# Converting three pairs of first-layer weights at double width, earlier, with the attention's slots moved around it

## The chip, the core and the metric

One core of a Trainium2 chip runs the whole program. The metric is the device time of one execution in microseconds. Three runs of the kernel before are known, and one more execution was profiled.

## What is computed

A chunked attention, then two gated layers one after the other:

```python
# attention: 4 batches x 8 heads x 768 positions, head width 64,
# chunks of 32 queries see 8 memory keys and up to 56 neighbouring keys
out = softmax(q @ k.T / 8) @ v
x = out as 3072 tokens x 512
# first layer (d_ff 1024)
h = (x @ w1) * (x @ w2)
y = (h @ w3) @ w_out
# second layer (d_ff 1536)
return ((y @ w_a) * (y @ w_b)) @ w_out2
```

The weights arrive as 64-bit floats, each as two 32-bit words.

## The kernel before

The program has three stages on one core, and five engines share it: TensorE (PE) multiplies, VectorE (DVE), ScalarE (ACT) and GpSimd (POOL) do the rest, SyncE (SP) starts most transfers. Each engine works off its instructions strictly in the order in which the program issued them, and that order is written out by hand.

**The weights' phase** multiplies w3 by w_out once, so that the first layer needs only one matrix after the gate. It has two halves of four accumulator banks. Each half loops over `k` from 0 to 5 and inside over `m` from 0 to 3, then over `m` with `k` 6 and 7 together. When a bank is complete, `w_evict` (line 568) splits it into a high part (ACT) and a low part (DVE) in `wsm`. All four banks of a half must be evicted before the next half reuses them.

**The first layer** runs in six tiles of 512 tokens. `ab_step` forms eight gated blocks per tile (matmuls into `psA` and `psB`, a product `gv`, a high part on ACT, a low part on POOL), then four outputs `psY`. After each group of twelve matmuls `between` (line 643) is called: 24 steps per tile (`NB`).

**The second layer** follows in tiles, with weights that the earlier steps converted and stored.

Into the first two stages two other streams are woven.

The *conversion*: `w_tick` (line 409) advances a pipe of weight blocks by one stage. An item is loaded by SP (`w_load`), scaled by two ACT instructions (`w_scale`), assembled by three DVE instructions (`w_bits`, lines 383 to 385), and, for the first layer's weights, split into a high part (ACT, line 419) and a low part (DVE, line 413). One tick does the low part of one item, the high part of the next, the assembly of the one behind it and the scaling of the fourth. The plan holds 12 items of w3 and w_out, each 1024 wide, and then 16 items of w1 and w2, each 512 wide; a pair `m` is two of these. There are three ticks ahead of the weights' phase, eight in each half, and the rest happen one per step in the first tile.

The *attention*: 64 units `u` of 96 queries and four heads. `attn_slot` works off numbered slots. Unit u has its scores (`sc`, PE) in slot 3u, the maximum (`mx`, DVE) in 3u+1, the exponentials (`t`, ACT, line 209) in 3u+2, the sum's reciprocal (`sm`, DVE) and the normalisation (`t`, POOL, line 222) in 3u+3. Its transposition (`pt`, PE) lies in `trans_slot(u)`, the copy to `p` (ACT, line 234) one slot later; for odd units the product with v (`xp`, PE) and the split into the layer's input `xt` (ACT and DVE) follow one and two slots after that, or with `e` = 1 one later still. `NEED[i]` is the slot number by which tile i's input is complete: 42, 72, 102, 138, 168, 198. Within a tile the slots are spread over the 24 steps between `NEED[i]` and `NEED[i+1]`.

Slots in the second half, by (k, m), before: k 0: 19, 20 | 21, 22; k 1: 23 | 24, 25; k 2: 26, 27 | 28, 29; k 3: 30 | 31, 32; k 4: 33, 34 | 35, 36; k 5: 37 | 38, 39; then 40 and 41. Left of the bar stands what is issued after `m` = 1, right of it what is issued after `m` = 3, behind that step's tick. Counted from the first, tick 12 is the one at k 0 and tick 17 the one at k 5; ticks 18 and 19 stand with k 7.

Loads of units up to 13 are started by POOL (`queue_of`), later ones by SP, where they stand in line with the weight loads.

Of the kernel before, what the change touches and what calls it, by code (L numbers as in the profile page):

```python
# [7 lines left out]
F32 = mybir.dt.float32  # L8
F32R = mybir.dt.float32r
U32 = mybir.dt.uint32  # L10
# [3 lines left out]
P = 128  # L14
# [10 lines left out]
NPLAIN = 22  # L25
NEARLY = 14
# [3 lines left out]
KD = DM // P  # L30
M1 = DF1 // P
M2 = DF2 // P
NEG = -1.0e30
CH = 512
BUFS = {"raw64": (3, 0), "raw2": (0, 3), "dec": (2, 4)}
A0 = (1, 2)
TB = 2

# [5 lines left out]
def tile_attention_moe(  # L44
# [21 lines left out]
    wpool = ctx.enter_context(tc.tile_pool(name="wpool", bufs=8))  # L66
    xpool = ctx.enter_context(tc.tile_pool(name="xpool", bufs=2))
    stagestack = ExitStack()
    stage = stagestack.enter_context(tc.tile_pool(name="stage", bufs=2))
    p0stack = ExitStack()  # L70
    p0 = p0stack.enter_context(tc.tile_pool(name="p0", bufs=3))
# [203 lines left out]
    def trans_slot(u):  # L275
        return 3 * u + 5 + max(0, (NEARLY - 2 - u) // 2)

    def slots_of(u):
        t, e = trans_slot(u), int(u < NEARLY - 4)
        return (  # L280
            (t + 3 + e, a_x),
            (t + 2 + e, a_pv),
            (t + 1, a_pt),
            (t, a_trans),
            (3 * u + 3, a_norm),
            (3 * u + 2, a_exp),
            (3 * u + 1, a_max),
            (3 * u, a_scores),
        )
# [7 lines left out]
    acount = [-3]  # L297
    NSLOT = 3 * (NU - 1) + 9

    NEED = [3 * (2 * -(-TT * (i + 1) // GQ) - 1) + 9 for i in range(NT1)]  # L300

    def attn_slot(n=1):
        for _ in range(n):
            s = acount[0]
            if s >= NSLOT:
                return
            acount[0] += 1
            for _, u, stage_of in sorted(todo.get(s, []), key=lambda x: x[:2]):
                stage_of(u)

            if s % 3 == 1 and s // 3 + 1 > NPLAIN + 1:
                a_prep_lo(s // 3 + 1)
            if s % 3 == 2 and s // 3 + 2 > NPLAIN + 1:
                a_prep_hi(s // 3 + 2)
            if s % 3 == 0 and NPLAIN <= s // 3 + 1 <= NPLAIN + 1:
                a_prep_hi(s // 3 + 1)
            if s % 3 == 1 and NPLAIN <= s // 3 + 1 <= NPLAIN + 1:
                a_prep_lo(s // 3 + 1)
            if s % 3 == 0 and s // 3 + 2 >= NPLAIN + 2:
                a_load(s // 3 + 2)  # L320
            if s % 3 == 2:
                if s // 3 + 2 <= NPLAIN + 1:
                    a_load(s // 3 + 2)

    plan = []
    for k in range(8):
        plan += [("w3a", k, 0, w3a[k].rearrange("p a c -> p (a c)"))]
    c12 = [("w12", m, c, w12[m, :, c]) for m in range(M1) for c in range(2)]  # L330
    for k in range(4):
        plan += [("w3b", k, 0, w3b[k].rearrange("p a c -> p (a c)"))]
    plan += c12
    wsrc = [x[3] for x in plan]
    size = [1 if x[0] == "w12" else 2 for x in plan]
    NW0 = max(i for i, x in enumerate(plan) if x[0] == "w3b") + 1
    wraw = []
    nload = [0]

    turn = {tag: [0, 0] for tag in BUFS}  # L340
    live = {tag: [0, 0] for tag in BUFS}

    def w_tile(i, tag, shape):
        x = int(tag == "raw2")
        if i < NW0 and tag == "dec":

            x = int(turn[tag][1] * BUFS[tag][0] < turn[tag][0] * BUFS[tag][1])
        n = BUFS[tag][x]
        if live[tag][x] == n:
            return None, x  # L350
        turn[tag][x] += 1
        live[tag][x] += 1
        return (stage, p0)[x].tile(shape, U32, tag=tag, bufs=n, name=tag), x

    def w_load():
        i = nload[0]
        if i < len(wsrc):
            tag = "raw64" if size[i] == 1 else "raw2"
            r, x = w_tile(i, tag, [P, size[i] * CH, 2])
            if r is not None:  # L360
                for c in range(2 if i == 0 else 1):
                    n = size[i] * CH // (2 if i == 0 else 1)
                    nc.sync.dma_start(
                        out=r[:, n * c : n * c + n, :].rearrange("p c w -> p (c w)"),
                        in_=wsrc[i][:, 2 * n * c : 2 * n * c + 2 * n],
                    )
                nload[0] += 1
                wraw.append((i, r, tag))
                return True
        return False  # L370
# [20 lines left out]

    def w_sum(i, r):
        kind, f = plan[i][:2]
        if kind == "w12":
            a, ax = w_tile(i, "dec", [P, CH])
            w_bits(a, r)
            return a.bitcast(F32), ax
        if f % 2 == 0:
            pairs["f"] = wpool.tile([P, 2, 2 * CH], U32, tag="w12", name="w3_f")
        a = pairs["f"][:, f % 2, :]  # L400
        for a1, r1 in halves_of(i, a, r):
            w_bits(a1, r1)
        if kind == "w3a":
            w3k[f], wo_f[f] = a[:, :CH], a[:, CH:]
        else:
            w3k[8 + 2 * f], w3k[9 + 2 * f] = a[:, :CH], a[:, CH:]
        return None, None

    def w_tick():

        if len(pipe[2]):
            i, a, ax, (d, f, w, hi, lo) = pipe[2].pop(0)
            nc.vector.tensor_tensor(lo, a, hi.bitcast(F32), ALU.subtract)
            live["dec"][ax] -= 1
            d[f] = w
        if pipe[1]:
            i, a, ax = pipe[1].pop(0)
            t = w_place(*plan[i][:3])
            nc.scalar.activation(t[3], a, AF.Copy)
            pipe[2].append((i, a, ax, t))  # L420
        if len(pipe[0]):
            i, r, tag = pipe[0].pop(0)
            a, ax = w_sum(i, r)
            live[tag][int(tag == "raw2")] -= 1
            if ax is not None:
                pipe[1].append((i, a, ax))
        if wraw:
            i, r, tag = wraw.pop(0)
            for (r1,) in halves_of(i, r):
                w_scale(r1)  # L430
            pipe[0].append((i, r, tag))
        while w_load():
            pass
# [8 lines left out]

    def w_place(kind, m, c):

        if c == 0:
            pairs[kind] = wpool.tile([P, 2, 2 * CH], F32R, tag="w12", name="w12")
        w = pairs[kind][:, :, CH * c : CH * (c + 1)]
        v = pairs[kind].rearrange("p l (k j f) -> p l k j f", k=KD, j=2)
        return (w12s if c else {}), m, v, w[:, 0, :], w[:, 1, :]
# [118 lines left out]
    def w_evict(half, m):  # L568
        w = wsm[4 * half + m] = w_new(wpool, "wo")
        nc.scalar.activation(w[:, 0, :], banks[m], AF.Copy)  # L570
        nc.vector.tensor_tensor(w[:, 1, :], banks[m], w[:, 0, :].bitcast(F32), ALU.subtract)
# [3 lines left out]
    for half in range(2):  # L575
        banks = [psd.tile([P, 512], F32, tag="d", name="wps") for _ in range(4)]
        for k, m in order:
            mm(
                banks[m],
                w3k[8 * half + k].bitcast(F32)[:, P * m : P * m + P],  # L580
                wo_f[k].bitcast(F32),
                k == 0,
                k == 7,
            )
            if k < 6 and m % 2 == 0 or k == 6:
                continue

            if half == 0:
                if m == 1 or k == 7 and m == 3:
                    w_tick()  # L590
                attn_slot(A0[m // 2] * (k > 0) if k < 6 else 1)
            else:
                if k < 6:
                    if m == 3:
                        w_tick()
                    attn_slot(1 + (m == 3 or k % 2 == 0))
                else:
                    if m % 2 == 1:
                        w_tick()
                    if m < 2:  # L600
                        attn_slot()
            if k == 7 and m > 0:
                w_evict(half, m - 1)
        w_evict(half, 3)
    nc.sync.dma_start(out=mask_sb, in_=mask)
    del pairs["f"]
    wo_f.clear()
# [16 lines left out]
    def ab_step(w, rhs, g2, between):  # L624
# [11 lines left out]
        nc.scalar.activation(g2[:, 0, :], gv, AF.Copy)  # L636
        nc.gpsimd.tensor_tensor(g2[:, 1, :], gv, g2[:, 0, :].bitcast(F32), ALU.subtract)  # L637

    nstep = [0]

    NB = 2 * M1 + 2 * KD

    def between():
        nstep[0] += 1
        if any(pipe) or wraw:
            w_tick()
        else:
            n = 1
            if ti == NT1 - 1:
                b = nstep[0] - NB * ti  # L650
                n = 2 if b <= 2 * M1 - 1 else 3 * (2 * M1 < b <= 2 * M1 + 5)
            for _ in range(n):
                next(cw, None)
        if ti < NT1 - 1:
            b = nstep[0] - NB * ti
            attn_slot(NEED[ti] + (NEED[ti + 1] - NEED[ti]) * b // NB - acount[0])


    def tmp():
# [357 lines left out]
```

## Time and profile before

| what | value |
|---|---|
| runs | 1124.27, 1123.73, 1122.76 us; median 1123.73 |
| profiled execution | 1123.1 us, span 1121.3 us |
| PE busy | 1100.3 us, 98% of the span |
| DVE, ACT, POOL busy | 624.8, 515.7, 296.0 us |
| granted TensorE clock, mean | 0.995 |

The span is what the trace covers; the profiled execution's time is 1.8 us longer. Busy shares are averages over all stages. A granted clock of 1.00 is 2.4 GHz, 0.50 is 1.2 GHz.

### The profile page before, as it was taken

What the parts mean: (1) busy time and instruction counts of PE and PEld (TensorE: products, weight loads), DVE (VectorE), ACT (ScalarE), POOL (GpSimd) and SP (SyncE); (2) the same over time, 40 slices, a digit from 0 to 9 for tenths busy, and PEclk for the clock granted to TensorE, in tenths of its full rate; (3) what the DMA queues carried; (4) which work ended last, traced back from release to release, by engine and by line L of the source; (5) the groups of instructions that cost most, each with busy time, mean ns of one, the idle gap of its engine ahead of it and who ended that gap; (6) DMA issues with size and microseconds to landing.
All of it is one profiled execution on the core that took longest, in us unless ns stands there. A gap on an engine that the chain in (4) does not pass through costs nothing.

```text
span 1121.3 us, 15493 instructions
## 1 busy us (share of the span) xinstructions
PE 1100.3 (98%) x5354; PEld 876.6 (78%) x5354; DVE 624.8 (56%) x1342; ACT 515.7 (46%) x1299; POOL 296.0 (26%) x308
## 2 busy tenths in 40 slices
PE   8899999999999999999999999999999999999998
PEld 3456877877887878877877878888888888888887
DVE  7879955876986876855865564252232243222220
ACT  6777756666775756644543334232222223222210
POOL 3452232331331322311212233202233211232210
PEclk9999999999999999999999999999999999999999
DMA  8845445345345444436546455434334352344311
GB/s 304 282 126 175 123 150 181 122 141 184 115 146 191 134 142 150 148 113 198 176 163 234 169 188 192 170 99 169 132 137 180 143 178 91 145 143 186 132 38 37
DMA packets 61671, 174.55 MB, mean 156 GB/s; under 512 B 8022, under 2 KB 18080, under 8 KB 55577
## 3 DMA queue, kind: packets, MB, share of 16 engines
q1 hardware_dynamic: 48762, 102.38, 27.4%
q0 software_dynamic: 12544, 70.91, 17.6%
q8 instruction: 42, 0.69, 0.3%
q14 instruction: 36, 0.29, 0.1%
q10 hardware_dynamic: 287, 0.27, 0.1%
HBM read 139.97 MB, written 33.55 MB: 155 GB/s over the span
## 4 chain that ended last, share of the span: by engine, by line
PE 77%; DVE 3%; issue 3%; ACT 3%; DMA 1%; POOL 1%; DVEq 0%; ACTq 0%; POOLq 0%; SPq 0%
PE ps L803 29%; PE ops L92 17%; PE psA L92 10%; PE psB L92 9%; PE psY L92 9%; PE sc L92 2%; PE xp L92 1%; PE pt L230 1%; DMA wc<-co 1%; ACT t L209 1%; DVE dec L384 1%; POOL g L637 0%; POOL t L222 0%; ACT xt L143 0%; ACT q L143 0%
## 5 line engine op out<-in xcount | busy, mean ns | idle before, releaser
L803 PE MATMUL ps<-x,w 128*128 128x512 f32 x1512 | 349.5, 390 | 3.8 <-ACT tmp L815 3.8
L803 PEld LDWEIGHTS ps<-x,w 128*128 128x128 f32 x1512 | 283.4, 188 | 64.6 <-ACT tmp L815 5.9
L820 DVE TENSOR_TENSOR tmp<-ps,tmp 128x512 f32<-128x512 f32 x108 | 74.6, 690 | 245.3 <-PE ps L803 241.3
L92 PE MATMUL psA<-xt,w 128*128 128x512 f32 x576 | 146.6, 402 | 1.9 <-ACT xt L143 1.2
L92 PE MATMUL psY<-g,wo 128*128 128x512 f32 x576 | 139.8, 394 | 1.5 <-POOL g L637 1.5
L92 PE MATMUL psB<-xt,w 128*128 128x512 f32 x576 | 141.0, 393 | 0.0
L702 POOL DMA_DIRECT2D w<-wc x72 | 40.0, 557 | 369.3 <-PE ps L803 369.2
L815 ACT ACTIVATE tmp<-ps 128x512 f32<-128x512 f32 x108 | 64.4, 596 | 147.4 <-PE ps L803 145.2
L92 PEld LDWEIGHTS psA<-xt,w 128*128 128x128 f32 x576 | 107.1, 191 | 26.9 <-ACT xt L143 2.3
L92 PEld LDWEIGHTS psY<-g,wo 128*128 128x128 f32 x576 | 105.4, 188 | 23.6 <-POOL g L637 2.9
L92 PEld LDWEIGHTS psB<-xt,w 128*128 128x128 f32 x576 | 105.5, 188 | 21.0
L92 PE MATMUL ops<-wo,g 128*128 128x512 f32 x504 | 118.6, 389 | 0.0
L637 POOL TENSOR_TENSOR g<-gv,g 128x512 fp32r<-128x512 f32 x48 | 65.8, 1371 | 199.5 <-ACT g L636 199.4
L222 POOL TENSOR_TENSOR t<-t,sm 96x512 f32<-96x512 f32 x64 | 69.0, 1078 | 176.7 <-ACT k L143 81.2
L92 PEld LDWEIGHTS ops<-wo,g 128*128 128x128 f32 x504 | 94.6, 188 | 19.6
L826 ACT ACTIVATE g<-tmp 128x512 fp32r<-128x512 f32 x66 | 40.7, 633 | 130.1 <-DVE tmp L825 130.1
L827 POOL TENSOR_TENSOR g<-tmp,g 128x512 fp32r<-128x512 f32 x66 | 87.0, 1340 | 26.3 <-ACT g L826 25.6
L92 PE MATMUL ops<-fo,g 128*128 128x512 f32 x288 | 68.2, 389 | 0.0
L209 ACT ACTIVATE t<-t,mx 96x128 f32<-96x128 f32 x168 | 65.1, 390 | 5.6 <-DVE mx L194 5.6
L92 PE MATMUL wps<-w_f 128*128 128x512 f32 x128 | 60.9, 608 | 3.7 <-DVE w_f L385 1.9
L92 PEld LDWEIGHTS ops<-fo,g 128*128 128x128 f32 x288 | 54.1, 188 | 11.2
L636 ACT ACTIVATE g<-gv 128x512 fp32r<-128x512 f32 x48 | 30.2, 629 | 70.3 <-DVE gv L635 69.9
(83 smaller groups left out, 1303.9 us busy)
## 6 DMA issues: line engine op xcount, KB each, us to landing
w<-wc POOLq DMA_DIRECT2D x36, 1024.0 KB, 6.8
w<-wc POOLq DMA_DIRECT2D x36, 768.0 KB, 4.9
wc<-co SPq DMA_DIRECT2D x84, 256.0 KB, 2.5
raw<-in_wab SPq DMA_DIRECT2D x24, 512.0 KB, 4.3
kraw<-in_kt SPq DMA_DIRECT2D x42, 256.0 KB, 3.0
raw<-in_w SPq DMA_DIRECT2D x16, 512.0 KB, 4.1
raw<-in_w3a SPq DMA_DIRECT2D x7, 1024.0 KB, 8.8
vraw<-in_vw SPq DMA_DIRECT2D x50, 128.0 KB, 2.9
```

Source lines behind the costliest of these rows:

```text
L92: nc.tensor.matmul(o, lhsT=l, rhs=r, start=first, stop=last)
L209: nc.scalar.activation(t[:, h, :], src[:, h, :], AF.Exp, bias=mx[:, h : h + 1], scale=scale, accum_out=sm[:, h : h + 1],)
L222: nc.gpsimd.tensor_tensor(t, t, sm[:, :, None].to_broadcast([GQ, HH, KW]), ALU.mult)
L230: nc.tensor.transpose(pt[:, h, :], t[:, h, :], id_sb)
L636: nc.scalar.activation(g2[:, 0, :], gv, AF.Copy)
L637: nc.gpsimd.tensor_tensor(g2[:, 1, :], gv, g2[:, 0, :].bitcast(F32), ALU.subtract)
L702: nc.gpsimd.dma_start(out=t[:, c0:c1].bitcast(F32), in_=src[:, c0:c1])
L803: nc.tensor.matmul(ps, lhsT=w[:, i, a, k, :], rhs=xs[i][:, b, k, :], start=first and n == 0, stop=n == 5, skip_group_check=not first,)
L815: nc.scalar.activation(z, ps, AF.Copy)
L820: nc.vector.tensor_tensor(z, ps, y, ALU.add)
L826: nc.scalar.activation(g2[:, 0, :], z, AF.Copy)
L827: nc.gpsimd.tensor_tensor(g2[:, 1, :], z, g2[:, 0, :].bitcast(F32), ALU.subtract)
```

## The change

Three pairs of the first layer (`EARLY`, kind `w12p`) become three items 1024 wide, which use the wide raw buffers and two wide `dec2` buffers. The plan has 25 items in place of 28. The ticks keep their number up to the first tile; there, every third step has none. `w_evict` moves ahead of the tick and the slots of its step, and the last tick of the first half moves behind the last eviction. In the second half the slots become k 1: 23, 24 | 25, 26; k 2: 27 | 28, 29; k 4: 33 | 34, 35; k 5: 36, 37 | 38, 39. Units 12 to 19 get `e` = 1. The spread over the tiles goes by `AIM`: 42, 74, 106, 138. In the diff a line of dots marks what is left out (the bookkeeping of buffers).

```diff
-BUFS = {"raw64": (3, 0), "raw2": (0, 3), "dec": (2, 4)}
+BUFS = {"raw64": 3, "raw2": 3, "dec": 2, "dec2": 2}
+EARLY = 3
...
-        t, e = trans_slot(u), int(u < NEARLY - 4)
+        t, e = trans_slot(u), int(u < NPLAIN - 2 and u // 2 != NEARLY // 2 - 2)
...
-    for k in range(4):
-        plan += [("w3b", k, 0, w3b[k].rearrange("p a c -> p (a c)"))]
-    plan += c12
+    plan += [("w3b", k, 0, w3b[k].rearrange("p a c -> p (a c)")) for k in range(4)]
+    plan += [("w12p", m, 0, w12[m].rearrange("p a c -> p (a c)")) for m in range(EARLY)]
+    plan += [("w12", m, c, w12[m, :, c]) for m in range(EARLY, M1) for c in range(2)]
...
-            a, ax = w_tile(i, "dec", [P, CH])
+            tag = "dec" if size[i] == 1 else "dec2"
+            a = w_tile(tag, [P, size[i] * CH])
...
+        if kind == "w12p":
+            t = wpool.tile([P, 2, 2 * CH], F32R, tag="w12", name="w12")
+            v = t.rearrange("p l (k j f) -> p l k j f", k=KD, j=2)
+            return w12s, m, v, t[:, 0, :], t[:, 1, :]
...
+            if k == 7 and m > 0:
+                w_evict(half, m - 1)
             if half == 0:
-                if m == 1 or k == 7 and m == 3:
+                if m == 1:
                     w_tick()
...
-                    attn_slot(1 + (m == 3 or k % 2 == 0))
+                    attn_slot(2 if m == 3 or k in (0, 1, 5) else 1)
...
-            if k == 7 and m > 0:
-                w_evict(half, m - 1)
         w_evict(half, 3)
+        if half == 0:
+            w_tick()
...
+    AIM = list(NEED)
+    for i in (1, 2):
+        AIM[i] = NEED[0] + (NEED[3] - NEED[0]) * i // 3
...
         if any(pipe) or wraw:
-            w_tick()
+            if nstep[0] % 3:
+                w_tick()
...
-            attn_slot(NEED[ti] + (NEED[ti + 1] - NEED[ti]) * b // NB - acount[0])
+            attn_slot(AIM[ti] + (AIM[ti + 1] - AIM[ti]) * b // NB - acount[0])
```

## Rows read from the trace of the kernel before

**Rows 1.** The page's first part: busy us, share of the span, instructions.

```profile
PE 1100.3 (98%) x5354; PEld 876.6 (78%) x5354; DVE 624.8 (56%) x1342; ACT 515.7 (46%) x1299; POOL 296.0 (26%) x308
```

**Rows 2.** Busy by stretch: length, PE, PEld, DVE, ACT, POOL, granted clock, DMA share, GB/s.

```profile
53.20:55.00 1.80, 0.01 (x1) 0.02 (x1) 1.76 (x5) 0.46 (x2) 0.47 (x1) 1.00 1.00 331
55.00:80.00 25.00, 24.93 (x148) 14.59 (x148) 18.72 (x37) 17.06 (x59) 13.45 (x20) 1.00 0.45 142
80.00:95.00 15.00, 14.84 (x85) 8.41 (x84) 14.44 (x31) 14.23 (x44) 5.86 (x8) 1.00 0.56 180
109.00:111.40 2.40, 0.17 (x5) 0.00 (x0) 2.14 (x4) 2.35 (x5) 0.00 (x0) 0.84 0.63 204
111.40:117.00 5.60, 5.59 (x19) 4.41 (x20) 5.27 (x10) 3.34 (x10) 2.56 (x2) 0.50 0.54 167
```

**Rows 3.** PE's timeline: start, us, what, [idle before <-releaser].

```profile
31.66 1.54 PE L92 MATMUL sc<-kraw,qraw 67*96 67x128 f32 x8 [1.74 <-DVE mx L187]
33.00 3.16 PE L92 MATMUL wps<-w_f 128*128 128x512 f32 x4
...
36.33 1.91 PE L92 MATMUL wps<-w_f 128*128 128x512 f32 x4
...
54.98 1.98 PE L92 MATMUL wps<-w_f 128*128 128x512 f32 x4 [1.80 <-DVE wo L571]
...
63.91 1.88 PE L92 MATMUL wps<-w_f 128*128 128x512 f32 x4
65.72 0.88 PE L92 MATMUL xp<-p,vraw 128*64 128x96 f32 x16
...
85.98 0.50 PE L230 MATMUL pt<-id_sb,t 96*128 96x96 f32 x4
...
95.03 3.31 PE L92 MATMUL psA<-xt,w 128*128 128x512 f32 x12
...
101.80 2.88 PE L92 MATMUL psA<-xt,w 128*128 128x512 f32 x12
...
111.41 0.91 PE L92 MATMUL xp<-p,vraw 128*64 128x96 f32 x8 [2.24 <-ACT p L234]
112.24 5.43 PE L92 MATMUL psA<-xt,w 128*128 128x512 f32 x12
...
141.97 0.55 PE L230 MATMUL pt<-id_sb,t 96*128 96x96 f32 x4 [0.38 <-POOL t L222]
...
184.16 3.42 PE L92 MATMUL psA<-xt,w 128*128 128x512 f32 x12 [0.36 <-ACT xt L143]
```

**Rows 4.** DVE's timeline in the weights' phase, same columns.

```profile
44.16 1.94 DVE L384 SCALAR_TENSOR_TENSOR w_f<-raw,w_f 128x1024 uint32<-128x1024 uint32 x1
...
56.24 0.68 DVE L383 TENSOR_SCALAR w_f<-raw 128x1024 uint32<-128x1024 uint32 x1
56.95 1.23 DVE L384 SCALAR_TENSOR_TENSOR w_f<-raw,w_f 128x1024 uint32<-128x1024 uint32 x1
...
59.36 0.16 DVE L220 TENSOR_SCALAR sm<-sm 96x4 f32<-96x4 f32 x1
...
74.29 0.17 DVE L220 TENSOR_SCALAR sm<-sm 96x4 f32<-96x4 f32 x1 [1.69 <-ACT t L209]
...
81.17 0.68 DVE L413 TENSOR_TENSOR w<-dec,w 128x512 fp32r<-128x512 f32 x1
81.88 0.43 DVE L383 TENSOR_SCALAR dec<-raw 128x512 uint32<-128x512 uint32 x1
...
83.68 0.16 DVE L220 TENSOR_SCALAR sm<-sm 96x4 f32<-96x4 f32 x1
```

**Rows 5.** ACT's timeline, same columns, in the weights' phase.

```profile
63.29 0.69 ACT L378 ACTIVATE raw<-raw 128x512 f32<-128x512 f32 x1
```

**Rows 6.** POOL's timeline, same columns, in the weights' phase.

```profile
43.72 1.30 POOL L222 TENSOR_TENSOR t<-t,sm 96x512 f32<-96x512 f32 x1 [0.17 <-DVE sm L221]
...
84.22 1.03 POOL L222 TENSOR_TENSOR t<-t,sm 96x512 f32<-96x512 f32 x1 [1.29 <-DVE sm L221]
```

More of the change, by code (lines that the diff above doesn't have):

```diff
@@ L323, in attn_slot, with w_tile @@
                     a_load(s // 3 + 2)
[L327 to L330, printed above, removed]
-    for k in range(4):
-        plan += [("w3b", k, 0, w3b[k].rearrange("p a c -> p (a c)"))]
-    plan += c12
+    plan = [("w3a", k, 0, w3a[k].rearrange("p a c -> p (a c)")) for k in range(8)]
+    plan += [("w3b", k, 0, w3b[k].rearrange("p a c -> p (a c)")) for k in range(4)]
+    plan += [("w12p", m, 0, w12[m].rearrange("p a c -> p (a c)")) for m in range(EARLY)]
+    plan += [("w12", m, c, w12[m, :, c]) for m in range(EARLY, M1) for c in range(2)]
     wsrc = [x[3] for x in plan]
     size = [1 if x[0] == "w12" else 2 for x in plan]
-    NW0 = max(i for i, x in enumerate(plan) if x[0] == "w3b") + 1
     wraw = []
     nload = [0]
[L340 to L353, printed above, removed]
+    live = {tag: 0 for tag in BUFS}
+    def w_tile(tag, shape):
+        n = BUFS[tag]
+        if live[tag] == n:
+            return None
+        live[tag] += 1
+        pool = p0 if tag[-1] == "2" else stage
+        return pool.tile(shape, U32, tag=tag, bufs=n, name=tag)
     def w_load():
@@ L358, in w_load @@
             tag = "raw64" if size[i] == 1 else "raw2"
-            r, x = w_tile(i, tag, [P, size[i] * CH, 2])
+            r = w_tile(tag, [P, size[i] * CH, 2])
             if r is not None:
@@ L393, in w_sum @@
         kind, f = plan[i][:2]
-        if kind == "w12":
-            a, ax = w_tile(i, "dec", [P, CH])
+        if kind in ("w12", "w12p"):
+            tag = "dec" if size[i] == 1 else "dec2"
+            a = w_tile(tag, [P, size[i] * CH])
             w_bits(a, r)
-            return a.bitcast(F32), ax
+            return a.bitcast(F32), tag
         if f % 2 == 0:
@@ L413, in w_tick @@
             nc.vector.tensor_tensor(lo, a, hi.bitcast(F32), ALU.subtract)
-            live["dec"][ax] -= 1
+            live[ax] -= 1
             d[f] = w
@@ L423, in w_tick @@
             a, ax = w_sum(i, r)
-            live[tag][int(tag == "raw2")] -= 1
+            live[tag] -= 1
             if ax is not None:
```

## The prediction

> **What bounds the kernel now.** I read the page's first part first. PE is busy for 1100.3 of 1121.3 us [rows 1], and the change alters none of its matmuls, so only two things can move the end: time in which PE stands idle, and time in which it runs at the lower clock. So I next followed PE's own timeline for its waits. From the start of the second half of the weights' phase to the second tile it shows four that matter [rows 3]: 1.80 us at 53.2, where the reused bank waits for the low part of an eviction; 2.24 us before 111.41, where the product with v waits for ACT's `p`; 0.38 us before the transposition at 141.97; 0.36 us before the second tile's `psA` at 184.16. The third view, busy time by stretch, gives the clock: 0.50 from 111.4 to 117 [rows 2], that is 1.2 GHz, right after the idle of 2.24 us. Twelve `psA` matmuls then take 5.43 us where the same twelve took 2.88 at 101.80 [rows 3], so that stall costs 2.24 + 2.55 = 4.8 us in all. At 31.66, after 1.74 us of idle, four `wps` instructions take 3.16 us instead of 1.91 [rows 3]: 1.25 us more. After the 1.80 us at 53.2 the clock did not fall [rows 2].
>
> The same view says who makes PE wait. DVE is busy for 18.72 of 25 us from 55 to 80 and for 14.44 of 15 us from 80 to 95 [rows 2]: it has room in the front part of the second half, none in the back part. What PE needs from DVE there is the softmax chain: scores, DVE's maximum, ACT's exponentials, DVE's sum, POOL's normalisation, PE's transposition. The lead is small: POOL ends unit 11's normalisation at 84.22 + 1.03 = 85.25 [rows 6], PE transposes it at 85.98 [rows 3]: 0.73 us.
>
> **The half's boundary.** With the evictions in front, bank 2's low part is no longer behind a wide assembly (3.12 us, worked out below) and a reciprocal in DVE's queue; so the 1.80 us goes away. But I count nothing for it. In the second half, slots 25 and 26 are now issued after k 1, m 3; PE reaches unit 5's product with v two matmul pairs earlier. Before, it stood at 65.72. Without the stall (1.80) and without the four `wps` instructions that came ahead of it (65.72 - 63.91 = 1.81) that is 62.1 [rows 3]. It needs unit 5's `p`, which follows unit 7's exponentials on ACT. These end at 63.29, where the next scaling starts [rows 5], and they hang on DVE's queue, which was full from 43.5 to 62 and loses nothing by a new order of the same work. `p` must still follow, so PE waits at least 63.29 - 62.1 = 1.2 us. What was late at the boundary is late here.
>
> **The wide items in the second half.** Ticks 14, 15 and 16 now assemble 1024 columns. Wide assembly: from 56.24 to the next instruction at 59.36, 3.12 us; narrow: 81.88 to 83.68, 1.80 us [rows 4]. Each of the three ticks gains 3.12 - 1.80 = 1.32 us on DVE. A narrow low part is 81.17 to 81.88, 0.71 us [rows 4]. A wide one isn't in the trace; joining two assemblies saved 2 x 1.80 - 3.12 = 0.48 us over three instructions, 0.16 each, so I take 2 x 0.71 - 0.16 = 1.26 (bounds 0.71 and 1.42). Tick 16 holds the first: +0.55. Up to unit 11's normalisation (slot 36) DVE thus has 3 x 1.32 + 0.55 = 4.5 us more work.
>
> The slots move too. Where a unit's sum stands right behind its maximum in DVE's queue, DVE idles for the exponentials in between: 1.69 us at 74.29 [rows 4]. Before, tick 13 stood between the two for unit 7, and tick 16 for unit 11. After, slots 22 to 24 have no tick between maximum 7 and sum 7, and slots 34 to 36 none between 11 and 11. Two new idles. The least each can cost is nothing (if ACT is early), the most 1.69; I take 1.5, near the row, since ACT has nothing else to wait for. DVE is then 4.5 + 3.0 = 7.5 us later at unit 11's sum. PE has 0.73 us of lead there, and from that transposition to the phase's end it has the same work in both orders, so the end of the phase goes from 95.03 to about 101.8: **+6.8 us**. On the way PE stands still in some three or four places (units 5, 9 and 11). ACT gains as much work, but it isn't what ends last at unit 11.
>
> The bounds: with no new idle, 4.5 - 0.73 = +3.8. With two of 1.69, and three wide assemblies that each meet a POOL instruction (1.94 us against 1.23 for line 384 at 44.16 and 56.95, +0.71 [rows 4]) where the narrow ones did not, 4.5 + 3.4 + 2.1 - 0.7 = +9.3.
>
> One rule speaks against the change. POOL's normalisation took 1.30 us at 43.72, beside a wide assembly, and 1.03 at 84.22 [rows 6]; I leave this 0.27 out. The Trainium skill ("SBUF — State Buffer", section "Who interferes with whom") says that VectorE and GpSimd share a port pair as an exclusive lock, which the first to start keeps for its whole instruction. By that rule a wide assembly could hold back the normalisation for 1.23 us where a narrow one holds it for 0.69, and the sum would rise by up to 3 x 0.54 = 1.6 us (an estimate from this page's rule). The 1.30 us agrees that the two engines meet; no row shows a hold as long as 1.23.
>
> **The clock.** Idles of about 2 us repeated in this half can drop it. The price of one drop lies between 1.25 and 2.55 us (above), or nothing as at 53.2. Drops ahead of a later wait are hidden by that wait; the one after unit 11's transposition, 9 us before the phase's end, isn't. I take **+1.8 us**.
>
> **The first tile.** Ten narrow assemblies and twelve low parts become seven and nine, and steps 3, 6, 9 and 12 have no tick. Before, slots 45 and 46 fell in one step, so unit 13's product with v stood right behind its `p`. With `e` = 1 it moves to slot 47; `AIM` (32 slots in 24 steps) puts 44 and 45 in step 3 and 47 in step 5. Two more groups of matmuls, about 6 us, lie between. The 2.24 + 2.55 = **-4.8 us** should come back. If ACT's backlog were larger by more than this, the stall would stay (bound: 0). The 0.38 at 141.97 goes since ticks have ended by then, and the 0.36 at 184.16 since slot 71 now stands a step earlier: **-0.7 us**, at least nothing. Two slots more in this tile only move PE work from the third.
>
> Costed at nothing: the wide loads (SP starts each two ticks ahead, as with the w3 items now), the step's delay of the second layer's weights (the stored blocks have tiles of time), the extra slot for units 12 to 19 (units 10, 11, 20 and 21, which end a tile, keep `e` = 0). SP's loads of units 14 and 15 stand behind a weight load that waits for tick 17's and 18's assembly; they are later by DVE's delay, like PE itself; without that cover, a score would wait.
>
> **The sum.** +6.8 + 1.8 - 4.8 - 0.7 = +3.1 us on the profiled execution's 1123.1: 1126.2. The median shown is 0.6 above it, so 1126.8 to compare with 1123.73: +0.27%. Differences under 0.2% (2.2 us) a measurement of this kernel can hardly tell from none.
>
> **Rivals.** *Faster.* DVE fills the room that it has before 80 (25 - 18.72 = 6.3 us [rows 2]) and is late by 3 us or less at unit 11. Then the phase ends at +2.3 at most, PE keeps its clock, and with -5.5 the run is at 1120.5 or below; if all of the delay is absorbed and the boundary's 1.8 stays gained, 1116.4. For it: the room is there and the slots are thinned at k 2 and k 4. Against: most of that room is waits of DVE for ACT, which two more adjacent pairs lengthen. It decides where the delay at unit 11 falls below 4.0 (4.0 - 0.73 = 5.5 - 2.2). The Trainium skill ("VectorE: DVE Perf Modes", section on the TRN2 errata) says that an instruction from SBUF pays a fixed cost once, however wide; by its formula for fp32, some 0.16 us for each of 12 joined instructions, an estimate of 1.9 us less DVE work in all. The trace agrees (0.16 above), but the saving falls mostly in the tile. Chance 0.28.
>
> *No change to be told.* The phase ends 3.8 to 6.8 later but the clock stays up: +6.8 - 5.5 = +1.3, 1125.0; with the lower bound -1.7, 1122.0. It needs the two idles or the drop to be absent. Chance 0.25.
>
> *Much slower.* DVE and ACT enter the first tile so late that unit 13's product stalls again, or another in its place: +3.1 + 4.8 = +7.9, 1131.6. DVE's delay must still be over 6 us at step 5. Against it: the ticks left out free about 2.5 us each (0.71 + 1.80). Chance 0.08.
>
> My forecast, slower by 2.2 to 7, has 0.39 and is the likeliest. Faster 0.28, same 0.25, slower 0.47. The range reaches from 1119.0 (leaving out half of the faster case) to 1131.5; the forecast's own is 1125.9 to 1130.7.
>
> **What would show it.** Right: no PE wait at the half's boundary, but one of 1 to 2 us before unit 5's `xp`; PE waiting for `t` or `p` at units 9 and 11; first `psA` near 102; a granted clock below 1.00 between 60 and 105; no stall at unit 13's `xp`. Wrong: first `psA` before 98, or DVE without idle between maximum and sum at units 7 and 11; or a stall of 2 us in the first tile.

## The result, and the profile after

The changed kernel is slower: 1130.01 us (median of 6 runs, 1128.60 to 1130.92) against 1123.51, a ratio of 1.0055 with a 95% interval of 1.0042 to 1.0068. The forecast was 1126.8, slower by 0.27%, with a range from 1119.0 to 1131.5. The profiled execution of the changed kernel was the slowest of its six (1130.92), and that of the kernel before lay 0.4 us below its median, so the two profiles lie 7.8 us apart where the medians lie 6.5.

The page's first part of the changed kernel says that PE did the same work and stood idle longer; DVE did less work, not more.

```profile
span 1129.1 us, 15470 instructions
PE 1098.9 (97%) x5354; PEld 874.6 (77%) x5354; DVE 615.2 (54%) x1330; ACT 514.7 (46%) x1290; POOL 294.2 (26%) x308
```

DVE's 9.6 us less than before [rows 1] didn't shorten the run. The place is in PE's timeline of the changed kernel (start, us, what, idle before and what ended it):

```profile
50.80 1.04 PE L93 MATMUL sc<-kraw,qraw 67*96 67x128 f32 x8
...
61.69 0.52 PE L231 MATMUL pt<-id_sb,t 96*128 96x96 f32 x4 [2.53 <-ACT p L235]
...
64.74 0.88 PE L93 MATMUL xp<-p,vraw 128*64 128x96 f32 x16
...
82.21 0.52 PE L231 MATMUL pt<-id_sb,t 96*128 96x96 f32 x4 [2.55 <-ACT p L235]
...
89.25 1.88 PE L93 MATMUL wps<-w_f 128*128 128x512 f32 x4
94.71 0.55 PE L231 MATMUL pt<-id_sb,t 96*128 96x96 f32 x4 [3.58 <-POOL t L223]
95.09 1.82 PE L93 MATMUL sc<-kraw,qraw 67*96 67x128 f32 x8
96.70 2.82 PE L93 MATMUL wps<-w_f 128*128 128x512 f32 x4
...
105.48 3.33 PE L93 MATMUL psA<-xt,w 128*128 128x512 f32 x12
...
130.35 0.55 PE L231 MATMUL pt<-id_sb,t 96*128 96x96 f32 x4 [0.84 <-POOL t L223]
...
138.62 0.55 PE L231 MATMUL pt<-id_sb,t 96*128 96x96 f32 x4 [0.51 <-POOL t L223]
...
190.09 2.89 PE L93 MATMUL psA<-xt,w 128*128 128x512 f32 x12
```

The wait at the half's boundary and the one before unit 13's product with v are gone [rows 3], and the first tile has two small ones (0.84 and 0.51). But PE waits 2.53, 2.55 and 3.58 us for units 5, 9 and 11 inside the second half, and after the last of these the scores took 1.82 us and four `wps` instructions 2.82, where 1.04 and 1.88 stand a few lines up. The busy view of that stretch shows why (length, PE, PEld, DVE, ACT, POOL, granted clock, DMA share, GB/s):

```profile
94.70:99.50 4.80, 4.79 (x18) 3.00 (x18) 4.33 (x9) 2.86 (x11) 1.88 (x3) 0.64 0.24 71
```

The granted clock is 0.64 on average, part of the stretch at 1.2 GHz. The first `psA` comes at 105.48 instead of 95.03: +10.45. The first tile then takes 84.61 us (to 190.09) instead of 89.13 (95.03 to 184.16 [rows 3]): -4.5. What is left is +5.9 at the second tile, and 7.8 at the span's end.

DVE's timeline of the changed kernel names the cause of the last two (unit 5's has another, which the run with the evictions alone shows):

```profile
64.27 0.17 DVE L221 TENSOR_SCALAR sm<-sm 96x4 f32<-96x4 f32 x1 [1.71 <-ACT t L210]
...
72.04 0.66 DVE L375 TENSOR_SCALAR dec<-raw 128x1024 uint32<-128x1024 uint32 x1
72.73 1.95 DVE L376 SCALAR_TENSOR_TENSOR dec<-raw,dec 128x1024 uint32<-128x1024 uint32 x1
74.71 1.23 DVE L377 CUSTOM_DVE_ANT_0 dec<-raw,dec 128x2048 uint16<-128x2048 uint16 x1
75.86 0.68 DVE L187 TENSOR_REDUCE mx<-sc 96x4 f32<-96x512 f32 x1
...
78.43 0.17 DVE L221 TENSOR_SCALAR sm<-sm 96x4 f32<-96x4 f32 x1 [1.69 <-ACT t L210]
...
85.11 0.17 DVE L221 TENSOR_SCALAR sm<-sm 96x4 f32<-96x4 f32 x1 [1.23 <-ACT t L210]
...
85.40 1.19 DVE L406 TENSOR_TENSOR w<-dec,w 128x1024 fp32r<-128x1024 f32 x1
86.63 1.42 DVE L375 TENSOR_SCALAR dec<-raw 128x1024 uint32<-128x1024 uint32 x1
...
93.07 0.17 DVE L221 TENSOR_SCALAR sm<-sm 96x4 f32<-96x4 f32 x1 [1.71 <-ACT t L210]
```

A sum (`sm`) with no conversion between it and its maximum waits for the exponentials: four times here, for units 7, 9, 10 and 11. Before, there were two, the 1.69 at 74.29 [rows 4] and 1.23 for unit 10. Unit 11's sum, the last line, starts at 93.07; before it started at 83.68 [rows 4]. A wide assembly takes 72.04 to 75.86 = 3.82 us: POOL's normalisation, released by the sum just ahead of it, runs at the same time (from 72.29, for 1.30 us), and line 376 took 1.95. The narrow assembly in the same place had met it too, as DVE's timeline of the kernel before shows, and took 69.20 to 71.69 = 2.49 us:

```profile
69.20 0.39 DVE L383 TENSOR_SCALAR dec<-raw 128x512 uint32<-128x512 uint32 x1
69.63 1.41 DVE L384 SCALAR_TENSOR_TENSOR dec<-raw,dec 128x512 uint32<-128x512 uint32 x1
...
71.69 0.68 DVE L186 TENSOR_REDUCE mx<-sc 96x4 f32<-96x512 f32 x1
```

### The profile page after: what moved, and what is told of

Same layout as the page of the kernel before. It is cut to its first block, busy times and chain, and to the rows that moved or that the text cites. A ratio compares the mean times of both kernels' runs of the same rounds, so it can differ in the third digit from the quotient of the medians.

```text
span 1129.1 us, 15470 instructions
## 1 busy us (share of the span) xinstructions
PE 1098.9 (97%) x5354; PEld 874.6 (77%) x5354; DVE 615.2 (54%) x1330; ACT 514.7 (46%) x1290; POOL 294.2 (26%) x308
## 4 chain that ended last, share of the span: by engine, by line
PE 72%; DVE 8%; ACT 4%; issue 3%; DMA 1%; POOL 1%; SPq 0%; DVEq 0%; ACTq 0%; POOLq 0%
PE ps L806 29%; PE ops L93 17%; PE psY L93 8%; PE psA L93 7%; PE psB L93 7%; PE sc L93 2%; DVE dec L376 1%; PE xp L93 1%; PE pt L231 1%; DMA tmp<-yd 1%; DVE gv L634 1%; DVE dec L375 1%; DVE dec L377 1%; ACT t L210 1%; ACT raw L370 1%
## 5 line engine op out<-in xcount | busy, mean ns | idle before, releaser
L93 PE MATMUL psA<-xt,w 128*128 128x512 f32 x576 | 142.7, 396 | 0.9 <-ACT xt L144 0.6
L636 POOL TENSOR_TENSOR g<-gv,g 128x512 fp32r<-128x512 f32 x48 | 63.3, 1319 | 186.5 <-ACT g L635 186.0
L635 ACT ACTIVATE g<-gv 128x512 fp32r<-128x512 f32 x48 | 30.3, 631 | 85.7 <-DVE gv L634 85.7
```

What stands on the lines that cost most here:

```text
L93: nc.tensor.matmul(o, lhsT=l, rhs=r, start=first, stop=last)
```

## Experiments

Each run is timed beside the kernel before on the same chip; the ratio is to that. Its medians in the four groups of runs were 1123.5, 1123.8, 1123.9 and 1124.1 us.

**Wide items undone.**

```diff
-EARLY = 3
+EARLY = 0
...
-            if nstep[0] % 3:
-                w_tick()
+            w_tick()
```

> The changed kernel with the wide items undone alone: the three pairs are narrow again and every step of the first tile has its tick; slots, evictions, the later product with v and the even spread stay. Theory (VectorE's queue in the second half sets the phase's end, by work and by new idles): 5.9 us of the 9.2 us of delay at unit 11's sum go, the two idles between maximum and sum (3.2 us) stay; first psA near 99 in place of 105.5, and with the first tile's gain mostly kept 1124 to 1125. Rival (the new slots make PE ask too early, the wide work is hidden): hardly changed, 1129 to 1130.

Measured: 1126.93 us, 1.0028 (1.0018 to 1.0038). DVE's unit 11 sum and PE's first `psA` in this run:

```profile
88.30 0.17 DVE L221 TENSOR_SCALAR sm<-sm 96x4 f32<-96x4 f32 x1 [1.71 <-ACT t L210]
```

```profile
100.68 3.33 PE L93 MATMUL psA<-xt,w 128*128 128x512 f32 x12
```

So, with the new slots, the wide items cost 105.48 - 100.68 = 4.8 us of the half, and as much at unit 11's sum (93.07 - 88.30), where 5.9 was expected; the theory holds and the rival falls. The expected time was missed by 2 us: the first `psA` came 1.7 us later than expected, and the first tile's gain was lost (88.95 us), since with narrow items and a tick in every step a transposition there waits 4.17 us. Behind the first tile this run took 3.7 us less than the changed kernel.

**Old slots in the changed kernel.**

```diff
-                    attn_slot(2 if m == 3 or k in (0, 1, 5) else 1)
+                    attn_slot(1 + (m == 3 or k % 2 == 0))
```

> The changed kernel with the slots of the second half as before, all else kept. Theory: the two new idles of VectorE between maximum and sum of units 7 and 11 go, 3.2 us; first psA near 102, 1126.5 to 1127.5. Rival (slots alone are to blame): all of it goes, first psA near 95, 1120 or below. Rival (slots don't matter, only the work): 1130.

Measured: 1125.48 us, 1.0020 (1.0011 to 1.0028). The same two lines:

```profile
89.35 0.16 DVE L221 TENSOR_SCALAR sm<-sm 96x4 f32<-96x4 f32 x1
```

```profile
100.08 3.33 PE L93 MATMUL psA<-xt,w 128*128 128x512 f32 x12
```

With the wide items in place, the slots cost 5.4 us, more than the 3.2 of DVE's idles that were expected: the waits of DVE for ACT's exponentials between 51 and 105 us fall from 6.3 us in four places to 2.9 in two, and the lower clock behind unit 11 goes too. (It falls here behind unit 5's wait of 2.73 us, ahead of one of 2.74 for a score at 76.65.)

The two figures, 4.8 and 5.4, come to 10.2 of the 10.45, but they don't split it, since each was measured with the other part in place. In this half the run with the evictions alone, two runs further on, is the changed kernel with both undone (the later product and the spread act behind the half): its first `psA` comes at 96.88, already 1.85 us later than before. From there the wide items alone add 3.2 us, the slots alone 3.8, and both together 8.6. In DVE's queue the two simply add: unit 11's sum comes at 84.47 there, 89.35 with the wide items, 88.30 with the slots and 93.07 with both, and 4.9 + 3.8 is close to 8.6. At PE the first 1.7 us of any delay at unit 11 are taken by its lead, and with the new slots the lower clock behind unit 11 puts 1.7 us on again, with narrow items too.

**The later product with v alone, in the kernel before.**

```diff
-        t, e = trans_slot(u), int(u < NEARLY - 4)
+        t, e = trans_slot(u), int(u < NPLAIN - 2 and u // 2 != NEARLY // 2 - 2)
```

> The kernel before with the later product with v for units 12 to 19 alone. Theory: the wait of 2.24 us before unit 13's product with v and the 2.55 us of lower clock behind it go, nothing else moves: 1118.7 to 1119. Rival (the wait only moves to the transposition of unit 14 or to a score, since VectorE and ScalarE are late there anyway): 1122 to 1123.5.

Measured: 1125.36 us, 1.0012 (1.0003 to 1.0021): slightly slower. My theory of that stall fails, and the rival holds in kind: the wait moved, though to a later unit than it named, and the time lies above its 1122 to 1123.5. PE's timeline of this run, below it DVE's, and last DVE's line for the same sum, unit 17's, in the kernel before:

```profile
111.70 0.88 PE L92 MATMUL xp<-p,vraw 128*64 128x96 f32 x16
...
142.09 0.78 PE L230 MATMUL pt<-id_sb,t 96*128 96x96 f32 x4 [4.15 <-POOL t L222]
142.56 4.45 PE L92 MATMUL psA<-xt,w 128*128 128x512 f32 x12
```

```profile
140.19 0.16 DVE L220 TENSOR_SCALAR sm<-sm 96x4 f32<-96x4 f32 x1
```

```profile
138.95 0.16 DVE L220 TENSOR_SCALAR sm<-sm 96x4 f32<-96x4 f32 x1
```

The product at 111.70 no longer waits. But unit 17's transposition comes at 142.09, no earlier than before (141.97 [rows 3]). PE ran ahead, DVE's queue, with a tick in each step, didn't: PE stood 4.15 us there instead of 0.38, more than the 2.24 that went, and lost clock there too (4.45 us for twelve `psA`).

**Evictions in front alone, in the kernel before.**

```diff
+            if k == 7 and m > 0:
+                w_evict(half, m - 1)
             if half == 0:
-                if m == 1 or k == 7 and m == 3:
+                if m == 1:
                     w_tick()
...
-            if k == 7 and m > 0:
-                w_evict(half, m - 1)
         w_evict(half, 3)
+        if half == 0:
+            w_tick()
```

> The kernel before with the evictions ahead of tick and slots, and the last tick of the first half behind them, alone. Theory: the 1.80 us wait at the half's boundary goes, but PE waits as much more for unit 5, 9 or 10 within the half: 1123 to 1123.5. Rival (the gain stays): 1121.7.

Measured: 1126.38 us, 1.0026 (1.0017 to 1.0035), slower than theory and rival had it. The 1.80 us are gone, but PE's timeline of this run shows what they became; below it DVE's line for unit 11's sum:

```profile
61.31 0.63 PE L230 MATMUL pt<-id_sb,t 96*128 96x96 f32 x4 [2.66 <-ACT p L234]
61.73 3.54 PE L92 MATMUL wps<-w_f 128*128 128x512 f32 x4
...
96.88 3.31 PE L92 MATMUL psA<-xt,w 128*128 128x512 f32 x12
```

```profile
84.47 0.16 DVE L220 TENSOR_SCALAR sm<-sm 96x4 f32<-96x4 f32 x1
```

Unit 5's transposition waits until ACT has copied unit 4's, since both use the one bank `pt`. The wait is longer than the one removed, and after it four `wps` took 3.54 us instead of 1.88.

**Two slots moved, in the kernel before**, so that ticks 14 and 15 stand between maximum and sum.

```diff
-                    attn_slot(1 + (m == 3 or k % 2 == 0))
+                    attn_slot(3 if (k, m) == (3, 3) else 2 if m == 3 or k in (0, 4) else 1)
```

> The kernel before with two slots moved alone: at k 2 one slot and then two, at k 3 one and then three, so that ticks 14 and 15 stand between maximum and sum of units 8 and 9. Theory (VectorE's queue, work and idles, is what the first 140 us run on): two idles of VectorE (2.0 and 1.7 us) go, it enters the first tile some 3.5 us earlier, the wait before unit 13's product with v goes or shrinks: 1119.5 to 1121. Rival (those idles were room that nothing used): 1123 to 1124.

Measured: 1124.14 us, 1.0005 (0.9996 to 1.0014): no change; the rival holds. In this half the kernel before did not run on DVE's queue: the waits by engine between 51 and 105 us show that DVE, freed of its idle, waited for PE's scores instead.

```profile
DVE mx L186 <- PE sc L92: 2.6, 3, 1.2
```

In the first tile the wait before unit 13's product stayed, without the lower clock behind it, and unit 17's transposition waited 1.76 us instead of 0.38; the tile took 88.57 us instead of 89.13. PE's timeline of this run:

```profile
112.06 0.55 PE L92 MATMUL xp<-p,vraw 128*64 128x96 f32 x8 [2.21 <-ACT p L234]
112.54 3.02 PE L92 MATMUL psA<-xt,w 128*128 128x512 f32 x12
...
142.44 0.55 PE L230 MATMUL pt<-id_sb,t 96*128 96x96 f32 x4 [1.76 <-POOL t L222]
```

**The same, with both parts that gained nothing alone** (the diffs of the three runs above together).

> The same two slots moved, and both parts that gained nothing alone: evictions in front and the later product with v. Theory: with VectorE's queue 3.5 us shorter these parts can keep some of what they gave back: 1118 to 1120.5. Rival (each makes a new wait of its own): above the run with the two slots alone.

Measured: 1126.99 us, 1.0027 (1.0017 to 1.0038). The rival holds: PE waits 2.62 us at unit 5's transposition and 3.13 us at 145.0 in the first tile. Its first `psA`:

```profile
97.05 3.31 PE L92 MATMUL psA<-xt,w 128*128 128x512 f32 x12
```

**The changed kernel with these slots.**

```diff
-                    attn_slot(2 if m == 3 or k in (0, 1, 5) else 1)
+                    attn_slot(3 if (k, m) == (3, 3) else 2 if m == 3 or k in (0, 4) else 1)
```

> The changed kernel with the slots of the run before, so that every wide tick stands between a maximum and its sum. Theory: of VectorE's idles in the second half (8.9 us in the changed kernel) some 6 go, first psA near 98 in place of 105.5, the first tile keeps its gain: 1121 to 1124. Rival (the wide work alone holds the phase up, wherever it stands): 1125.5 as with the old slots, or more.

Measured: 1123.17 us, 0.9995 (0.9986 to 1.0004): some 7 us better than the changed kernel by one line, as expected, and level with the kernel before. First `psA` at 97.55, first tile 84.7. DVE's timeline of this run around a wide assembly:

```profile
73.00 0.68 DVE L375 TENSOR_SCALAR dec<-raw 128x1024 uint32<-128x1024 uint32 x1
...
76.12 0.16 DVE L221 TENSOR_SCALAR sm<-sm 96x4 f32<-96x4 f32 x1
...
80.46 0.17 DVE L221 TENSOR_SCALAR sm<-sm 96x4 f32<-96x4 f32 x1 [1.42 <-ACT t L210]
```

The sum behind the assembly at 73.00 has no wait (the exponentials ran meanwhile), and the assembly takes 3.12 us instead of 3.82, since POOL's normalisation starts behind it and not with it. One such idle is left, 1.42. So the rival that the wide work holds the phase up wherever it stands falls. The run before this one says the same: in this half it has the same slots and evictions with narrow items, and its first `psA` came at 97.05. With these slots the wide items cost 0.5 us of the half, where they cost 3.2 with the old slots and 4.8 with those of the change.

**The low parts on GpSimd, in the kernel before.**

```diff
-            nc.vector.tensor_tensor(lo, a, hi.bitcast(F32), ALU.subtract)
+            nc.gpsimd.tensor_tensor(lo, a, hi.bitcast(F32), ALU.subtract)
```

> The kernel before with the low part of the first layer's weights on GpSimd in place of VectorE, sixteen instructions. Theory: VectorE's queue is 0.71 us shorter per tick, 4 x 0.71 in the second half and 12 x 0.71 in the first tile; PE's waits of 4.8 us there go: 1119 to 1121. Rival (GpSimd, which also normalises, becomes late, and holds VectorE's instructions up where both read): 1124 to 1128.

Measured: 1136.82 us, 1.0115 (1.0101 to 1.0128), worse than either case. The waits of this run between 51 and 125 us:

```profile
DVE dec L383 <- POOL w L413: 9.1, 3, 3.3
...
PE xp L92 <- ACT p L234: 7.3, 1, 7.3
```

DVE's next assembly needs the buffer that the low part reads, so DVE now waits in line behind POOL. Moving work off a queue is no gain where the queue then waits for it.

**Slots apart**, in the changed kernel: also no transposition in one group with the copy that frees its bank.

```diff
-                    attn_slot(2 if m == 3 or k in (0, 1, 5) else 1)
+                    attn_slot({1: (2, 0, 1, 2, 2, 1), 3: (2, 3, 1, 3, 2, 2)}[m][k])
```

> The changed kernel with another order of the second half's slots: ticks 13 to 15 stand between maximum and sum, and the transpositions of units 5 and 7 no longer fall into the same group as the copy to p that frees their bank (k 1: none, three; k 2: one, one; k 3: two, three; k 4: two, two; k 5: one, two). Theory (what PE waits for is the queue of VectorE and ScalarE as the slots order it, not the wide work): PE's waits of 2.55 and 1.33 us that the aligned run still had go, first psA near 95, 1119.5 to 1121.5. Rival (they move on to a later unit): 1122.5 to 1124.

Measured: 1123.50 us, 0.9997 (0.9988 to 1.0006). The two waits shrink from 2.55 and 1.33 to 0.95 and 0.98, but a score now waits 1.55 us for its q to land; first `psA` at 96.91. The rival holds: the waits move on.

**Slots apart, old bounds, ticks left out at every fourth step**, and then each of the two alone.

```diff
-        AIM[i] = NEED[0] + (NEED[3] - NEED[0]) * i // 3
+        AIM[i] = NEED[i]
...
-            if nstep[0] % 3:
+            if nstep[0] % 4:
```

> The same, with a tick left out at every fourth step in place of every third, and the tiles' slots spread by the old bounds. Theory: the first tile keeps its gain (the ticks end at step 11 in place of 13), the second layer's start gets back some 0.6 us that it lost where the later weights began a step later, the second and third tile lose the waits of 0.9 and 0.6 us that the even spread brought: 1 to 2 us below the run beside it. Rival (denser ticks bring the first tile's wait back): 2 us or more above it.

> The apart run with the tiles' slots spread by the old bounds, ticks left out at every third step as in the change. It splits what failed when both were changed together. If the spread was to blame (36 slots in the third tile, where that run took 86.5 us from start to start against 82.5): 1127 or more, third tile near 86. If the denser ticks were: 1123 to 1124, third tile near 82.

> The apart run with a tick left out at every fourth step, the even spread kept. If the denser ticks and the earlier start of the second layer's weights were to blame: 1127 or more. If not: 1122.5 to 1124, as the apart run.

Measured: both 1130.02 us, 1.0056 (1.0045 to 1.0068); old bounds alone 1124.48, 1.0002 (0.9993 to 1.0010); every fourth step alone 1126.39, 1.0020 (1.0011 to 1.0029). The even spread is worth nothing: without it the third tile takes 85.7 us instead of 82.5, and the first two take 1.8 and 1.0 us less. Leaving out every third tick in place of every fourth is worth some 2.6 us (1.0020 against 0.9997). The two don't add up to the 6.5 us by which the run with both lies above the apart run; its profile, of its slowest execution (1132.86), has a wait of 3.48 us for unit 3's q at 33.35, where the other two wait 1.7 us, and whether its other executions have it stays open.

No version is faster than the kernel before. Four are level with it: itself with the two slots moved, and the changed kernel with these slots, with the slots apart, and with the slots apart and the old bounds.

## Why the forecast held, point by point

**The sign and the path** held: PE's end is set by the softmax chain through DVE, and the chain got later in the second half by more than the first tile gave back.

**The second half, +6.8 forecast:** unit 11's transposition went from 85.98 [rows 3] to 94.71, +8.7. The term was under-sized: DVE was 93.07 - 83.68 = 9.4 us later at unit 11's sum, not 7.5. The two new idles took 1.71 each (1.5 assumed): 0.4 more. DVE also entered the half late, with unit 7's maximum at 61.68 instead of 60.92: 0.8 for a reordering that I had counted as nothing. And two assemblies met POOL's normalisation that had not met it before, 0.7 each: the last w3 item, which now stands behind unit 7's sum, and that of tick 16. I had kept this price for the bound of +9.3, and there I misread the narrow assemblies: those of ticks 14 and 15 did meet a POOL instruction (2.49 us, not 1.80), so there a wide one at 3.82 cost the 1.3 us that I had counted and nothing on top. These add up to 2.6; some 0.7 of it was given back by shorter stretches between the other maxima and sums. The wide low part took 1.23 us to the next start; 1.26 was assumed.

**The clock, +1.8:** from that transposition to the first `psA` 105.48 - 94.71 = 10.8 us passed, before 95.03 - 85.98 = 9.05: +1.7.

**The boundary, nothing gained:** right, by the wrong step of unit 5. Unit 5's product with v waited for nothing at 64.74; its transposition, one slot earlier, waited 2.53 us for the single bank `pt`, which I had not looked at. The run with the evictions alone shows the same wait.

**The first tile, -4.8 and -0.7:** measured -4.5. The amount was about right by luck, for the reason given was not. I credited the later product with v; alone it gives nothing. The tile is shorter where it also has fewer blocks and fewer ticks on DVE (84.61 us in the changed kernel, 88.95 with narrow items and all ticks); whether these would do it without the later product was not run. The two small waits did not go either: 0.84 and 0.51 us stand in place of 0.38 and 0.36.

**Not in the sum:** +1.9 us behind the first tile, part of the 7.8 between the two profiles. From the second tile's first `psA` to the end of the span it took 937.1 us before and 939.1 after, and I had counted this stretch as nothing. The runs separate two effects in it. With narrow items and the even spread (the first experiment) it took 935.4; with wide items and the old bounds (slots apart, old bounds alone) 941.1. So the even spread gives some 2 us back here, and the wide items with the ticks left out for them cost 3.7, most of the 4.3 that they give in the first tile (88.95 against 84.61). About 1.0 of the 3.7 lies in the second layer, whose weights are converted a step later; whether that is the cause I did not settle.

**The rivals:** *faster* failed as its own argument against it said: the room before 80 us was mostly waits. *No change* failed since both idles and the drop were there. *Much slower* came near by its number, 1131.6 against 1130.01, and not by its mechanism: no stall stood in the first tile, and the half was later than forecast instead. The forecast of the ratio, 1.0027, was about half of 1.0055.

The Trainium skill's rule on the shared port pair ("SBUF — State Buffer", section "Who interferes with whom") spoke against the change, and the trace agrees that the two hold each other up: line 376 took 1.95 us beside POOL's normalisation and 1.23 without. The price worked out from it, up to 0.54 us per wide assembly on POOL's side, was not the one paid. VectorE was held by 0.7, and the narrow assemblies had been held by as much (1.41 us instead of 0.69), so only where the order changed did it cost anything. POOL's normalisations took 1.30 us twice and 1.83 once for units 8 to 10, but unit 11's, on which PE's transposition hung, took 1.03 as before.

## What to carry to other kernels

In this kernel a stall of the busiest engine was worth its length only if the queue that it waits for got shorter too. Where two engines take turns, look for what stands between a producer's step and its consumer's in the slower queue: one line that puts a conversion between a maximum and its sum was worth 7 us here, more than any removed stall. Judge each part alone as well as together; two that remove a visible wait were each a little slower alone.

## What the runs showed of the hardware

The clock doesn't follow the length of one idle: 1.74 us before 31.66 in the kernel before was followed by the lower clock [rows 3], 1.74 at 31.77 in the apart run by scores of 1.08 us at full clock; 2.24 us before unit 13's product in the kernel before was followed by it [rows 3], 2.21 at the same place with the two slots moved wasn't; 2.66 us (evictions alone) was, 2.53 at 61.69 in the changed kernel wasn't. So a stall of about 2 us cost PE its length alone, or 1.25 to 2.55 us on top.

Beside POOL's normalisation VectorE's second assembly instruction took some 0.7 us longer at either width: 1.41 instead of 0.69 at 512 columns, 1.95 instead of 1.23 at 1024. And a GpSimd subtraction of 128x512 took 1.28 us where VectorE's took 0.68.
